# Joining the value products of an attention stage with the scores of the stage after next, in a kernel whose instruction order a planner writes

## The chip, the cores and the metric

The kernel runs on one core of one Trainium2 chip. The metric is the time of one execution on the device in microseconds (us); runs of one kernel are summed up by their median. A profiled execution gives, beside its own time, the span from the first to the last instruction and a record of each instruction on each engine.

## The reference

Local attention with block summaries, followed by a feed-forward network (FFN), all in float32:

```python
batch, n_heads, seq, head_dim = (4, 8, 768, 64); block, window = (32, 16)
k_sum = k.reshape(B, H, nb, block, D).max(axis=3)          # nb = 24 blocks
v_sum = v.reshape(B, H, nb, block, D).mean(axis=3)
scores_l = where(abs(pos_q - pos_k) < window, scale * q @ k.T, -1e9)
scores_s = scale * q @ k_sum.T + log(block)
a = softmax(concat([scores_l, scores_s]))
x = a @ concat([v, v_sum])                                  # 3072 tokens x 512
h = x @ w_in                                                # 512 -> 2048
out = (h * sigmoid(h)) @ w_out                              # 2048 -> 512
```

## The kernel before, in words

**Tiling.** The 3072 tokens make 24 attention *stages* of 128 tokens (`s`, six to a batch) and 12 FFN *chunks* of 256 tokens (`c`, two stages to a chunk). For each of the 16 slices `f` of the 2048 hidden columns a chunk has one product into the hidden layer (FFN1) and two out of it (FFN2, one per 128 tokens). Chunk 0 computes in float32 (FFN1 at L818, in halves at L840; FFN2 at L826). Later chunks split each operand in two float16 parts, an upper (`h`) and a lower (`l`), and add three products: FFN1 at L821, FFN2 at L829. Chunk 10 uses a scheme with seven instead of eight products of a block (L917, L948).

**An attention stage.** `job_scores` (L581) multiplies q and k into two PSUM banks (L594; in batch 0 L597 and L601 in float32). `job_a` masks and reduces on VectorE (L630), takes the exponential on ScalarE (L633), divides by the sum (L638 to L648), and turns the weights: in batch 0 by TensorE (L659) and a copy on ScalarE or VectorE (L234, L238, the lines of the helper `copy`), later by a DMA transpose (L680). `job_c` multiplies by the values into bank 7 (L712; L697 in batch 0), and `job_x` copies the result to `x`, the FFN's input (L728, L729; in chunk 0 by the helper `copy`). From stage 4 on, all scores go to the banks 6 and 3.

**Preparation.** For each batch from the second on, `job_k` and `job_scale` load k and q to find a scale (L369, L371, L389), `job_v` loads v for its block means and its maximum (L455, L457), and for each stage `job_qk` and `job_vs` load and convert q and k (L489 to L496) and v (L556 to L566). The loads go through three staging tiles `raw` in turn, so that the order in which jobs ask for a tile is the order in which loads become possible. The FFN's weights arrive packed; ScalarE and VectorE unpack them in chunk 0 (L754 to L760) and VectorE takes their maximum (L761). When the maxima of all slices are there, `w_scale` computes a scale: a transposition by TensorE (L784), six small steps on VectorE (L788 to L793), a broadcast by TensorE (L797) and a copy (`ws`, L798). Then `job_pair` converts two slices at once to the upper part (L774 on ScalarE, L775 on VectorE) and the lower part (L776). Chunk 1 can't begin its FFN1 before that.

**What sets the order.** None of these jobs issues its instructions at once. Each hands operations to `Plan` with the engines that can run them, an assumed cost for each, what they read and write, and an urgency. `Plan.schedule` simulates the five queues (TensorE, VectorE, ScalarE, GpSimd, and SyncE, which issues all DMAs) with these assumed costs, sweeps a few times backward and forward to find urgencies, and keeps the order that is shortest by its own account. That order is then issued, engine by engine; each engine works its queue in order and waits at an instruction whose inputs aren't there. `plan.slack` adds time to what an engine has to wait for by the plan. `TUNE` holds offsets of urgencies. Where the plan sees TensorE idle before chunk 0, or before an FFN1 block later, it inserts *fillers*, small bf16 products of an identity tile whose result nobody reads (L328).

## Time and profile before

| | us |
|---|---|
| median of 3 runs | 596.81 |
| lowest and highest run | 596.72, 597.51 |
| the profiled execution's own time | 597.37 |
| its span, first to last instruction | 595.7 |
| first float32 FFN1 matmul of chunk 0 (L840) starts | 24.90 |
| first float16 FFN1 matmul of chunk 1 (L821) starts | 88.55 |
| last matmul (L859) starts | 591.76 |

PE stands for TensorE's matmuls, PEld for its loads of weights, DVE for VectorE, ACT for ScalarE, POOL for GpSimd and SP for SyncE. In the rows of the timeline the first number is the start in us from the span's start, the second how long the group took, "x12" the number of instructions, and a bracket at the end the idle time before them and what ended it. Matmuls are pipelined, so that one is still recorded as busy while the next has begun: the distance from start to start tells what one costs. In a group's row the numbers behind the bar are the busy time of all in us and the mean of one in ns.

### The profile page before, as it was taken

How to read it: one execution, taken by the hardware profiler on the slowest of the kernel's cores; microseconds unless marked ns; L12 is line 12 of the kernel's file. 1: busy time of each engine (PE TensorE's matmuls, PEld its weight loads, DVE VectorE, ACT ScalarE, POOL GpSimd, SP SyncE). 2: the span in 40 equal slices, each digit the busy share in tenths (PEclk: the TensorE clock that was granted, in tenths of full speed). 3: DMA queues.
4: the chain of work that ended last, by engine and by line, in shares of the span. 5: the costliest groups of instructions: out<-in, count | busy, mean ns of one | idle time of the engine just before them, and what ended most of it. 6: DMA issues, size and time to landing. Idle time of an engine off the chain costs nothing.

```text
span 595.7 us, 15528 instructions
## 1 busy us (share of the span) xinstructions
PE 585.4 (98%) x5920; PEld 407.1 (68%) x5920; DVE 454.1 (76%) x1348; ACT 384.6 (65%) x1030; POOL 152.7 (26%) x221
## 2 busy tenths in 40 slices
PE   7999999999999999999999999999999999999997
PEld 5666656676676666666676766666666767788764
DVE  5999979998786848979895564988987896655432
ACT  4898849877766756647775643767876765533332
POOL 3211201035412000033331010236236637421000
PEclk9999999999999999999999999999999999999999
DMA  8999443125755633553555620344733321000000
GB/s 333 414 417 413 169 133 99 28 61 179 145 114 178 166 93 104 111 145 88 129 123 153 198 90 2 129 89 128 163 80 85 103 46 38 19 2 19 37 1 35
DMA packets 60918, 75.30 MB, mean 126 GB/s; under 512 B 41915, under 2 KB 42171, under 8 KB 59051
## 3 DMA queue, kind: packets, MB, share of 16 engines
q1 hardware_dynamic: 60842, 74.31, 42.3%
q8 instruction: 46, 0.75, 0.6%
q14 instruction: 30, 0.24, 0.1%
HBM read 56.79 MB, written 6.29 MB: 106 GB/s over the span
## 4 chain that ended last, share of the span: by engine, by line
PE 83%; DVE 9%; ACT 3%; DMA 3%; issue 1%; SPq 0%; ACTq 0%
PE bank L821 34%; PE bank L829 34%; PE bank L917 4%; PE bank L948 3%; PE bank L712 2%; PE bank L594 2%; DVE wm L761 2%; DVE wr L760 2%; DMA second<-in_qP_dram 1%; DVE e L630 1%; ACT wr L774 1%; DMA third<-first 1%; ACT wr L758 1%; PE bank L840 1%; DMA raw<-in_qF_dram 1%
## 5 line engine op out<-in xcount | busy, mean ns | idle before, releaser
L821 PE MATMUL bank<-x,wr 128*128 128x256 f16 x1920 | 234.6, 273 | 0.0
L821 PEld LDWEIGHTS <-wr 128*128 128x128 f16 x1920 | 186.7, 98 | 50.6 <-issue 0.6
L829 PE MATMUL bank<-wr,gh 128*128 128x512 f16 x638 | 190.1, 379 | 0.0
L845 ACT ACTIVATE t<-bank,th 128x256 f32<-128x256 f32 x160 | 75.0, 469 | 83.2 <-PE bank L821 82.3
L846 DVE SCALAR_TENSOR_TENSOR t<-t,bank 128x256 f32<-128x256 f32 x176 | 73.6, 418 | 68.8 <-ACT t L845 67.8
L829 PE MATMUL bank<-wr,gl 128*128 128x512 f16 x319 | 120.9, 379 | 0.2 <-DVE gl L849 0.2
L848 ACT ACTIVATE gh<-t 128x256 f16<-128x256 f32 x160 | 66.1, 414 | 52.6 <-DVE t L846 47.8
L849 DVE SCALAR_TENSOR_TENSOR gl<-t,gh 128x256 f16<-128x256 f32 x160 | 75.8, 474 | 24.1 <-ACT gh L848 23.0
L829 PEld LDWEIGHTS <-gh 128*128 128x128 f16 x638 | 60.0, 98 | 39.3
L633 ACT ACTIVATE e<-e,mx 128x120 f32<-128x120 f32 x192 | 73.1, 383 | 9.5 <-DVE mx L630 9.3
L829 PEld LDWEIGHTS <-gl 128*128 128x128 f16 x319 | 31.2, 98 | 39.2 <-DVE gl L849 2.1
L677 DVE SCALAR_TENSOR_TENSOR first<-e,sum,first 128x120 f16<-128x120 f32 x144 | 52.5, 411 | 0.0
L646 POOL TENSOR_SCALAR first<-e,sum 128x120 f16<-128x120 f32 x55 | 24.9, 462 | 96.5 <-ACT gh L848 29.8
L630 DVE CUSTOM_DVE_ANT_0 e<-bank,masks,qsc 128x120 f32<-128x120 f32 x144 | 42.0, 337 | 2.7 <-PE bank L594 2.7
L241 POOL TENSOR_TENSOR first<-raw,first 120x1024 f16<-120x1024 f32 x15 | 32.9, 2197 | 28.1 <-ACT first L234 27.2
L633 ACT ACTIVATION_READ_ACCUMULATOR e<-e,mx 128x1 f32 x192 | 36.4, 190 | 0.0
L826 PE MATMUL bank<-wr,t 128*128 128x512 f32 x64 | 30.7, 599 | 0.0
L646 POOL TENSOR_SCALAR e<-e,sum 128x120 f32<-128x120 f32 x28 | 11.2, 413 | 73.3 <-DVE sum L639 63.4
L241 POOL TENSOR_TENSOR wr<-wr 128x256 f32<-128x256 f32 x32 | 25.2, 808 | 12.5 <-DVE wr L897 8.0
L818 PE MATMUL bank<-x,wr 128*128 128x256 f32 x112 | 26.3, 379 | 0.0
L818 PEld LDWEIGHTS bank<-x,wr 128*128 128x128 f32 x112 | 21.0, 190 | 7.0 <-issue 4.1
L917 PE MATMUL bank<-x,wr 128*128 128x256 f16 x192 | 22.4, 273 | 0.4 <-DVE wr L923 0.4
(164 smaller groups left out, 757.0 us busy)
## 6 DMA issues: line engine op xcount, KB each, us to landing
wr<-in_w_dram SPq DMA_DIRECT2D x14, 1024.0 KB
raw<-in_qkT_dram SPq DMA_DIRECT2D x18, 576.0 KB
out_dram<-raw SPq DMA_DIRECT2D x23, 256.0 KB
raw<-in_kF_dram SPq DMA_DIRECT2D x12, 384.0 KB
raw<-in_qF_dram SPq DMA_DIRECT2D x9, 512.0 KB
raw<-in_vR_dram SPq DMA_DIRECT2D x12, 384.0 KB
raw<-in_v_dram SPq DMA_DIRECT2D x18, 208.0 KB
raw<-in_v_dram SPq DMA_DIRECT2D x18, 192.0 KB
```

Source lines behind the costliest of these rows:

```text
L241: eng[e].tensor_tensor(out=out, in0=in0, in1=in1, op=ALU.subtract)
L630: plan.op({"dve": 262 if b else 206}, lambda e, i=i, j=j, et=et, mx=mx: nc.vector.tensor_tensor_reduce(out=et[:, i, :], in0=sc[j][:, i, :N ...
L633: plan.op({"act": 385}, lambda e, i=i, j=j, et=et, mx=mx: nc.scalar.activation(out=et[:, i, :], in_=et[:, i, :], func=AF.Exp, scale=-1.0, ...
L677: nc.vector.scalar_tensor_tensor(out=pt[:, i, P:P + NKEY], in0=et[:, i, :], scalar=su4[:, 2 * j + i:2 * j + i + 1], in1=pt[:, i, :NKEY], o ...
L818: nc.tensor.matmul(out=h, lhsT=wi[:, ct * P:(ct + 1) * P], rhs=x0[:, ct, :], start=(ct == 0), stop=(ct == NCT - 1))
L821: nc.tensor.matmul(out=h, lhsT=wip[:, part, ct * P:(ct + 1) * P], rhs=x[:, ct, :], start=(ct == 0 and q == 0), stop=(ct == NCT - 1 and q = ...
L829: nc.tensor.matmul(out=bank[ob[u]], lhsT=g[:, u * P:u * P + P], rhs=wop[:, part, :], start=(opens and q == 0), stop=(closes and q == 2))
L845: plan.op({"act": 264 if c == 0 else 360}, lambda e: nc.scalar.activation(out=t, in_=h, func=AF.Tanh, scale=0.5 if c == 0 else th[:, 0:1]) ...
L846: plan.op({"dve": 337}, lambda e: nc.vector.scalar_tensor_tensor(out=t, in0=t, scalar=1.0, in1=h, op0=ALU.add, op1=ALU.mult), r=bk(k), w=[ ...
L848: plan.op({"act": 311}, lambda e: nc.scalar.activation(out=gh, in_=t, func=AF.Copy, scale=SHRINK), r=[("t", j)], w=[("gh", n)], prio=post)
L849: plan.op({"dve": 343}, lambda e: nc.vector.scalar_tensor_tensor(out=gl, in0=t, scalar=SHRINK, in1=gh, op0=ALU.mult, op1=ALU.subtract), r= ...
L917: nc.tensor.matmul(out=h, lhsT=wip[:, p, ct * P:(ct + 1) * P], rhs=x[:, ct, :], start=(ct == 0 and q == 0), stop=(ct == NCT - 1 and q == 2))
```

## The change

1. **Joined products.** For stages 6 to 21 without the last two of each batch (twelve stages), `job_c` adds the value products of stage `s` and the scores of stage `s + 2` as one operation, so that nothing comes between them on TensorE. To make that possible, the jobs of a stage are written in another order: `step` hands in the softmax of the next stage, the loads of the stage after next, the joined operation and the rest of the loads; and `job_scale` of batches 2 and 3 comes later than `job_k`.
2. **First conversions one slice each.** `job_pair` converts the slices 0 to 3 singly, the others in pairs as before; for a pair the plan now knows that FFN1 of its second slice waits for both of its conversions (`near`).
3. **Landings.** Operations on VectorE and ScalarE that read a freshly loaded tile (L369, L371, L455, L457, and the upper parts of q and k) are planned as if the load landed 1300 ns later.
4. **Urgencies.** `TUNE` has other values, and 72 `MOVES` are applied behind the sweeps: each draws random shifts for the urgencies of the operations in a stretch of the plan and sweeps once more. `Plan.move` was there before, with an empty list.

```diff
+LANDING = 1300
-MOVES = ()
+MOVES = ((258747, 243766, 16000, 300, 8), (489776, 214955, 2000, 1500, 1),
...
+SINGLE = 4
...
+    @contextmanager
+    def landing():
+        saved = plan.slack
+        plan.slack = dict(saved, **{e: max(LANDING, saved.get(e, 0)) for e in ("dve", "act")})
+        yield
+        plan.slack = saved
...
-        plan.op({"pe": 770}, mm, r=[ttk for _, ttk in parts] + [("v1", s % 2), ("v2", s % 2)], w=bk(7), prio=prio, cols=1536, mode=2)
+        need = [ttk for _, ttk in parts] + [("v1", s % 2), ("v2", s % 2)]
+        if not joined(s):
+            plan.op({"pe": 770}, mm, r=need, w=bk(7), prio=prio, cols=1536, mode=2)
+            return
+        go, more, homes = scores(s + 2)
+        plan.op({"pe": 1450}, lambda e: (mm(e), go(e)), r=need + more, w=bk(7) + homes, prio=prio, cols=2976, mode=2)
...
+        near = [("near", f0)] if n > 1 else []
...
-        need = [("wf", f, 0)] if c == 0 else [("wh", f, 0), ("wl", f, 0)]
+        need = [("wf", f, 0)] if c == 0 else [("wh", f, 0), ("wl", f, 0)] + ([("near", f - 1)] if c == 1 and f % 2 and f > SINGLE else [])
...
+    def joined(s):
+        return s >= NTILE and s % NTILE < NTILE - 2
...
+    def step(s):
+        end = B * NTILE
+        if s + 1 < end:
+            job_as(s + 1)
+        if s + 2 < end:
+            if s % NTILE == NTILE - 2:
+                job_scale(s // NTILE + 1, when(4 * s + 8) - TUNE["k"])
+            job_stage(s + 2, False)
+        job_cs(s, True)
+        if s + 2 < end:
+            if not joined(s):
+                job_scores(s + 2, when(4 * s + 8))
+            job_rest(s + 2)
...
         for kind in range(2):
-            job_pair((f, f + 1), kind, NFT + f + kind - TUNE["wp"])
+            for fs in ((f,), (f + 1,)) if f < SINGLE else ((f, f + 1),):
+                job_pair(fs, kind, NFT + f + kind - TUNE["wp"])
...
         if d and c and f == 0:
-            job_stage(2 * d)
-            job_attn(2 * d, True)
-            job_stage(2 * d + 1)
+            if c == 1:
+                for x in (2 * d, 2 * d + 1):
+                    job_stage(x)
+                    job_scores(x, when(4 * x))
+                    if x == 2 * d:
+                        job_as(x)
+            step(2 * d)
```

`scores` is the inner part of `job_scores`, which now returns the products, what they need and their banks; `job_as`, `job_cs` and `job_rest` are parts of `job_attn` and `job_stage` under names of their own.

**What it moves.** The order of the new kernel has other line numbers: L712 is L733 there, L594 L607, L821 L848, L829 L856, L818 L845, L826 L853, L234 L236, L754 L780, L758 L784, L633 L651, L845 L872, L846 L873, L457 L468, L455 L466, L447 L457, L788 to L793 L815 to L820, L798 L825, L774 to L776 L801 to L803, L328 L330 (and L840 for the fillers of an FFN1 block). `first` holds the values, `second` q and k, `third` the turned weights.

On TensorE, before, an attention stage's scores (here those of stage 8) follow an FFN2 product:

```order
L829 LDWEIGHTS gl0_174
L829 MATMUL bank4_182<-wr_61,gl0_174 128x512
L594 LDWEIGHTS second_122
L594 MATMUL bank6_184<-second_122 64x120
L594 LDWEIGHTS second_122
L594 MATMUL bank3_181<-second_122 64x120
```

Now the same scores follow the last value products of stage 6:

```order
L733 LDWEIGHTS first_121
L733 MATMUL bank7_185<-third_123,first_121 64x64
L607 LDWEIGHTS second_122
L607 MATMUL bank6_184<-second_122 64x120
L607 LDWEIGHTS second_122
L607 MATMUL bank3_181<-second_122 64x120
```

So one change between FFN tiles and small tiles is gone; the order has this step twelve times.

On ScalarE, before, at the end of the start phase: copies of turned weights (`third`), the block means (`wr<-vms`), unpacking of FFN weights (`wr<-wr`), and divisions (`e<-e,sum`):

```order
L234 COPY third<-bank_180 120x256
L234 COPY wr<-vms 24x512
L234 COPY third<-bank_181 120x256
L234 COPY wr<-vms 24x512
L758 ACTIVATE wr<-wr 128x512
L644 ACTIVATE e_159<-e_159,sum_151 128x120 x2
L754 ACTIVATE wr<-wr 128x512
L758 ACTIVATE wr<-wr 128x512
L234 COPY third<-bank_183 120x256
L758 ACTIVATE wr<-wr 128x512
L754 ACTIVATE wr<-wr 128x512 x2
```

Now, with a copy of the attention's result to `x` that VectorE had before, and the tanh of the first FFN tile at the end:

```order
L662 ACTIVATE e_158<-e_158,sum_151 128x120
L236 COPY wr<-vms 24x512 x2
L236 COPY third<-bank_183 120x256
L780 ACTIVATE wr<-wr 128x512
L784 ACTIVATE wr<-wr 128x512 x3
L651 ACTIVATE e_160,sum_148<-e_160,mx_154 128x120 x2
L236 COPY x_164<-bank_185 128x4x128
L651 ACTIVATE e_161,sum_148<-e_161,mx_155 128x120 x2
L784 ACTIVATE wr<-wr 128x1024
L872 ACTIVATE t_166<-bank_178 128x256
```

All unpacking has moved behind the last copy of turned weights, and the copy to `x` stands behind four steps of it. On TensorE the scores of a stage that stood behind the second block of L697 stand ahead of it now.

On VectorE, before, around the scale of the FFN's weights (`wc`, `ws`), with the two reductions of v (`am`, `vm`) of the next batch:

```order
L789 TENSOR_SCALAR wc<-wc 1x2
L457 TENSOR_REDUCE am<-raw_119 128x1
L790 TENSOR_SCALAR wc<-wc 1x2
L455 TENSOR_REDUCE vm<-raw_119 128x24
L791 TENSOR_SCALAR wc<-wc 1x2
L846 SCALAR_TENSOR_TENSOR t_168<-t_168,bank_178 128x256
L792 RECIPROCAL wc<-wc 1x2
L793 SCALAR_TENSOR_TENSOR wc<-wc 1x1
L846 SCALAR_TENSOR_TENSOR t_169<-t_169,bank_179 128x256
L798 COPY ws<-bank_184 128x4
L447 TENSOR_TENSOR th_146<-ws,vsc_140 128x2
L775 TENSOR_SCALAR wr<-wr,ws 128x2x512 x2
```

Now:

```order
L819 RECIPROCAL wc<-wc 1x2
L820 SCALAR_TENSOR_TENSOR wc<-wc 1x1
L873 SCALAR_TENSOR_TENSOR t_168<-t_168,bank_178 128x256
L466 TENSOR_REDUCE vm<-raw_119 128x24
L468 TENSOR_REDUCE am<-raw_119 128x1
L825 COPY ws<-bank_184 128x4
L457 TENSOR_TENSOR th_146<-ws,vsc_140 128x2
L802 TENSOR_SCALAR wr<-wr,ws 128x512 x2
L803 SCALAR_TENSOR_TENSOR wr<-wr,ws 128x512
L802 TENSOR_SCALAR wr<-wr,ws 128x512
```

The reductions have left the chain of the small steps and stand ahead of the copy of the scale; the first conversions are of one slice (512 columns) instead of two.

More of the change, by code (lines that the diff above doesn't have):

```diff
@@ L2 @@
 import random
-from contextlib import ExitStack
+from contextlib import ExitStack, contextmanager
 import concourse.bass as bass
@@ L601, in go, with job_scores @@
                             nc.tensor.matmul(out=bank[both[u]][side[z], hp * P:hp * P + NKEY][:, means[z]], lhsT=q0_t[s % NQ0][rows, hp, side[z]], rhs=km0[rows, hp], start=True, stop=True)
+        need = [(x, s % 2) for x in ("qh", "ql", "kh", "kl", "km2")] if b else [("q0", s % NQ0)] + [(x, hp) for x in ("k0", "k0m") for hp in range(4)]
+        return go, need, bk(both[0]) + bk(both[1])
+    def job_scores(s, prio):
+        b, both = s // NTILE, score_banks(s)
+        go, need, homes = scores(s)
         if s < 2:
@@ L1015, in job_stage, with job_rest @@
                 job_mean(-TUNE["v0"])
-        job_vs(s, p[0] - TUNE["vs"] if b else p[0])
+        if rest:
+            job_rest(s)
+    def job_rest(s):
+        b, t = divmod(s, NTILE)
+        p = when(4 * s)
+        job_vs(s, p - TUNE["vs"] if b else p)
         if t == (4 if b else 5) and b + 1 < B:
```

58 lines of the change are left out of this document (35 added, 23 removed).

## Prediction

> **What bounds the kernel now.** I read the page first, then the windows, then what TensorE waited for, then the timeline at each place where it waited. The busy line of the page, three windows (us, busy us of PE, PEld, DVE, ACT, POOL, granted clock, DMA share, GB/s) and TensorE's own list of waits (us in total, times, longest):
>
> ```profile
> PE 585.4 (98%) x5920; PEld 407.1 (68%) x5920; DVE 454.1 (76%) x1348; ACT 384.6 (65%) x1030; POOL 152.7 (26%) x221
> 25.00:50.00 25.00, 25.00 (x109) 17.83 (x110) 23.88 (x51) 23.51 (x45) 2.47 (x7) 1.00 1.02 419
> 75.00:100.00 25.00, 23.64 (x174) 15.08 (x173) 20.84 (x52) 17.55 (x41) 0.00 (x0) 1.00 0.35 113
> 110.00:120.00 10.00, 10.00 (x69) 6.52 (x68) 10.00 (x22) 7.14 (x16) 0.00 (x0) 1.00 0.01 2
> 450.00:500.00 50.00, 50.00 (x581) 34.01 (x581) 39.08 (x115) 34.20 (x97) 31.71 (x37) 1.00 0.28 63
> PE bank L597 <- ACT raw L874: 1.0, 1, 1.0
> PE bank L697 <- ACT third L234: 0.8, 1, 0.8
> PE bank L917 <- DVE wr L923: 0.4, 1, 0.4
> PE bank L797 <- DVE wc L793: 0.4, 1, 0.4
> ```
>
> TensorE is busy for 98% of the span at a granted clock of 1.00, so nothing is to be had from the clock. From 100 us on it is gapless but for 0.4 us (L917). All that a new order can take back lies in three places: the first 25 us, before the first FFN matmul; three waits between 65 and 92 us (0.8 + 0.4 + 1.0 = 2.2 us); and what TensorE spends inside its busy time on work that isn't products. The set of products is unchanged by the change, so that last part is the cost of changing from one shape of tile to another, and of fillers.
>
> **Part one: joined values and scores.** Around one block of scores (L594, 64x64 tiles) and one of values (L712, 120x64 tiles) the timeline reads (start, us, engine, line):
>
> ```profile
> 186.13 0.38 PE L829 MATMUL bank<-wr,gh 128*128 128x512 f16 x1
> 186.35 0.38 PE L829 MATMUL bank<-wr,gl 128*128 128x512 f16 x1
> 186.66 0.82 PE L594 MATMUL bank<-second 64*64 64x120 f16 x48
> 187.42 1.81 PE L821 MATMUL bank<-x,wr 128*128 128x256 f16 x15
> ...
> 271.86 0.38 PE L829 MATMUL bank<-wr,gl 128*128 128x512 f16 x1
> 272.17 0.95 PE L712 MATMUL bank<-third,first 120*64 120x64 f16 x48
> 273.05 0.50 PE L821 MATMUL bank<-x,wr 128*128 128x256 f16 x3
> ...
> L712 PE MATMUL bank<-third,first 120*64 120x64 f16 x864 | 17.1, 197 | 0.0
> ```
>
> One L829 follows another after 0.22 us (186.13 to 186.35), but a block of small tiles follows an L829 only after 0.31 us (186.35 to 186.66, 271.86 to 272.17): entering costs 0.09 us, for scores and for values alike. A value block then holds TensorE for 0.88 us (272.17 to 273.05). Its 48 matmuls start over 0.95 - 0.20 = 0.75 us, some 0.02 us apart, so leaving costs 0.88 - 0.75 - 0.02 = 0.11 us. Before, a stage pays both entries and both exits. Joined, the entry into the scores from an FFN block goes for certain: 0.09 us. The step from 120x64 to 64x64 tiles has no row of its own for f16; it costs between nothing (then 0.11 us more is saved) and as much as the exit that it replaces. I take the exit's cost, since the shape of the tile changes there too. Twelve stages are joined (four in each of three batches): 12 x 0.09 = **-1.1 us**; bounds -1.1 and 12 x 0.20 = -2.4 us. [...]
>
> What the joined step adds: the scores of stage s+2 now stand right behind the values of stage s in TensorE's queue. They need the converted q and k of stage s+2, and both score banks read out by stage s+1. Were they late, all FFN blocks behind them would wait. I cost that at nothing, because two stages of FFN work lie between the joins and a wait of this kind isn't in the list above; it is the second rival.
>
> **Part two: the start.** From 19 us to the first FFN output product (L826):
>
> ```profile
> 21.28 0.66 ACT L754 ACTIVATE wr<-wr 128x512 uint32<-128x512 uint32 x1
> 21.84 0.71 ACT L758 ACTIVATE wr<-wr 128x512 f32<-128x512 f32 x1
> 22.43 0.34 ACT L234 COPY third<-bank 120x256 f32<-120x256 f32 x1
> 21.79 1.49 PE L697 MATMUL bank<-third,wr 120*64 120x64 f32 x32
> 23.20 0.40 PE L597 MATMUL bank<-first,second 64*64 64x96 f32 x8
> 24.90 2.94 PE L840 MATMUL bank<-x,wr 128*128 128x128 f32 x24
> 26.99 0.38 ACT L845 ACTIVATE t<-bank 128x256 f32<-128x256 f32 x1 [0.45 <-PE bank L840]
> 27.41 0.41 DVE L846 SCALAR_TENSOR_TENSOR t<-t,bank 128x256 f32<-128x256 f32 x1
> 29.08 1.88 PE L826 MATMUL bank<-wr,t 128*128 128x512 f32 x4
> 23.36 0.67 DVE L238 COPY x<-bank 128x512 f32<-128x512 f32 x1
> ...
> L633 ACT ACTIVATE e<-e,mx 128x120 f32<-128x120 f32 x192 | 73.1, 383 | 9.5 <-DVE mx L630 9.3
> L758 ACT ACTIVATE wr<-wr 128x1024 f32<-128x1024 f32 x14 | 16.3, 1164 | 0.0
> ```
>
> ScalarE has three steps of unpacking FFN weights (an L754 of 0.66 and two L758 like that of 21.84, 0.71: together 2.1 us) ahead of the last copy of attention weights (22.43) that stage 1's values (L697) wait for. The new order puts them behind that copy, and the scores block of 23.20 to 24.90 ahead of those values, where TensorE had been filling time. So the copy can end at 22.77 - 2.1 = 20.7, the values run from 20.8 to 21.9, and the first L840 starts at about 22.0 instead of 24.9. But the copy of stage 1's result to x moves from VectorE (23.36) to ScalarE, behind one L754, three L758 and two exponentials: 0.66 + 3 x 0.71 + 2 x 0.38 = 3.5 us, then 0.6 for the copy itself: 20.7 + 4.1 = 24.8. The second half of the L840s (two of four blocks of 2.94 / 3 = 1.0 us) waits for it and completes the first tile at 25.8. Then ScalarE has two exponentials and a wide L758 (1.16 us) ahead of the tanh, which starts at 26.7; with 0.38 + 0.41 us for tanh and product, L826 comes at 27.5 instead of 29.08: **-1.5 us**. Bounds: nothing (weights converted later, as VectorE at 23.88 of 25 us has no room), and the whole 2.9 us of the first L840.
>
> **Part three: the waits of 65 to 92 us.** VectorE, TensorE and ScalarE around the scale of the weights:
>
> ```profile
> 79.66 0.16 DVE L789 TENSOR_SCALAR wc<-wc 1x2 f32<-1x2 f32 x1
> 81.27 0.95 DVE L457 TENSOR_REDUCE am<-raw 128x1 f32<-128x768 f32 x1 [1.46 <-DMA raw<-in_vR_dram]
> 83.65 0.15 DVE L793 SCALAR_TENSOR_TENSOR wc<-wc 1x1 f32<-1x1 f32 x1
> 83.85 0.38 PE L797 MATMUL bank<-wc,ones 1*128 1x4 f32 x2 [0.36 <-DVE wc L793]
> 84.26 0.16 DVE L798 COPY ws<-bank 128x4 f32<-128x4 f32 x1
> 85.64 1.42 DVE L775 TENSOR_SCALAR wr<-wr,ws 128x1024 f16<-128x1024 f32 x2 [1.02 <-ACT wr L774]
> 86.97 6.31 DVE L776 SCALAR_TENSOR_TENSOR wr<-wr,ws 128x1024 f16<-128x1024 f32 x5
> 88.55 1.47 PE L821 MATMUL bank<-x,wr 128*128 128x256 f16 x12
> ```
>
> The six small steps from L788 to L793 last 4 us because two reductions of v (0.95 us each) stand between them, the first with 1.46 us of waiting for its load. The new order moves both behind L793, where they run beside the FFN block and the three L826 products that TensorE has between L784 and L797; so the 0.4 us at L797 go. From the copy of the scale (L798) to the first fp16 product 4.3 us pass now (84.26 to 88.55), with the upper parts of two pairs (1.42) and the lower part of one (6.31 / 5 = 1.26) ahead of it on VectorE. With one f each these are 2 x 0.36 and 0.63: with the copy 0.16 + 0.72 + 0.63 = 1.5 us. TensorE's own cover for it shrinks from five L826 products to three, six matmuls of 1.88 / 4 = 0.47 us by row 29.08, 2.8 us: enough, so no new wait comes in its place: **-0.4**. The wait of 0.8 at L697 has about the same cover as before (two L826 products, 1.9 us, instead of one FFN block), but ScalarE now has its copies in a row there: **-0.8**. At L597 (1.0) the eviction of the second bank on ScalarE still has conversions ahead of it, now two of one f instead of one of a pair, so I take half: **-0.5**. Sum **-1.7 us**, bounds 0 and -2.2.
>
> **Part four: what comes in its place.** The new order has four fillers ahead of one FFN block of chunk 1, where before had none after the start:
>
> ```profile
> 8.86 2.47 PE L328 MATMUL bank<-ident 128*128 128x256 bf16 x21
> ```
>
> They are 2.47 / 21 = 0.12 us each, 0.5 us. VectorE is busy for 10.00 of 10 us at 110 to 120, so when TensorE arrives some 3 us earlier, conversions can't all be earlier too; I add one wait like that of L917, 0.4 us, and round to **+0.8 us**, bounds 0 and +3.2 (all that parts two and three gain). The moves of urgencies and the 1.3 us allowed for landings shift work on engines that have idle time (VectorE 24%, ScalarE 35%) once chunk 1 is over, at 39.08 and 34.20 of 50 us; behind 130 us I cost them at nothing, cover being TensorE's own queue. If that cover is gone, it is the second rival again. The last block and the stores behind it are unchanged.
>
> Sum: -1.1 - 1.5 - 1.7 + 0.8 = -3.5 us. On the profiled execution's own 597.37 us that is 593.9; the median of the runs is 596.81, 0.56 lower, and gives **593.3 us**. The difference that a measurement of this kernel can tell from none is about 0.2%, 1.2 us: faster means under 595.6, slower over 598.0.
>
> **Rivals.**
> - *VectorE becomes the bound in chunk 1.* For it: 10.00 of 10 us, and 23.88 of 25 during chunk 0. Against it: 20.84 of 25 us from 75 to 100, of which 1.46 is the wait that goes. Then parts two and three (3.2 us) are given back but for about a third, and the result is -1.1 - 1.0 + 0.8 = -1.3: 595.5 us.
> - *The joined scores wait, slower.* Place: TensorE at the step from values to scores. Price: the upper and lower part of k are one conversion on ScalarE (0.82 us) and one on VectorE (0.92), rows below; if the load lands late these 1.7 us stand after it, the value block hides 0.75, so 1.0 us shows. It decides from 3.5 / 12 = 0.3 us a join on; at six of twelve joins it is +6.0 - 3.5 = +2.5: 599.3 us. For it: ScalarE already waits for that load (0.6 us in all). Against it: TensorE waits for none of these conversions now.
> - *All goes through.* Parts two and three at 2.5 and 2.2, no new wait: -1.1 - 2.5 - 2.2 = -5.8: 591.0 us, and 1.3 less where the step between small tiles is free.
> - *The change doesn't do what it says* falls: the order shows values and scores without a row between them.
>
> ```profile
> L492 ACT ACTIVATE second<-raw,qsc 128x640 f16<-128x640 f32 x15 | 12.3, 818 | 0.7 <-DMA raw<-in_qkT_dram 0.6
> L494 DVE SCALAR_TENSOR_TENSOR second<-raw,qsc,second 128x640 f16<-128x640 f32 x18 | 16.6, 922 | 0.5 <-ACT second L492 0.4
> ```
>
> **The numbers.** Forecast 0.57 (its own range 591.8 to 594.9), VectorE bound 0.20, joins wait 0.11, all goes through 0.12. Faster takes the forecast, all of the third and under half of the first rival (those below 595.6): 0.57 + 0.12 + 0.08 = 0.77; the rest of the first, 0.12, is the same; slower 0.11. The range reaches from the third rival with half of the free step (591.0 - 0.6) to joins alone with the fillers (596.81 - 1.1 + 0.5): 590.4 to 596.2, and leaves out the slower rival and the ends of the others.
>
> **What would show it.** Right: a first L840 near 22 and a first L826 near 27.5; no wait at L797 and L697; first fp16 product at about 85.5 instead of 88.55; 0.9 us from a joined block's first value to its first score. Free step: 0.77 us there. Wrong: waits of TensorE for second (q, k) or for score banks at the joins, or a list of TensorE's waits behind 92 us that sums to more than 2 us; or a start that moves by under 0.5 us.

## The result and the profile after

| | before | after |
|---|---|---|
| median of six runs, us | 596.87 | 601.47 |
| lowest and highest run, us | 596.19, 597.51 | 599.85, 602.21 |
| the profiled execution's own time, us | 597.37 | 599.85 |
| its span, us | 595.7 | 598.1 |
| first FFN2 product of chunk 0 starts | 29.08 | 28.27 |
| first FFN2 product of chunk 1 starts | 95.22 | 92.15 |
| from there to the last matmul starts | 496.55 | 502.10 |

The kernel became slower: ratio 1.007 [1.0056, 1.0084]. The forecast of 593.3 us and its range up to 596.2 both missed. Three of the six runs of after had a mean granted clock of 0.997 and were on average 1.6 us longer than the other three; the profiled one is the fastest, so what follows explains its 2.48 us (599.85 - 597.37) and not the whole distance of the medians. Of the experiments below, one execution of e6 (675.01 us) and one of e9 (865.34 us) ran at a mean granted clock of 0.849 and 0.657 and are left out of their medians and ratios.

The last three rows of the table split the change in two: up to chunk 1 the kernel gained 95.22 - 92.15 = 3.07 us, near the 3.2 us forecast for start and early waits together; behind it, it lost 502.10 - 496.55 = 5.55 us where the forecast had a gain of 0.3 (1.1 for the joins less the 0.8 of part four, whose fillers stand at 122 us and whose wait was expected at 110 to 120). So 5.55 + 0.3 = 5.85 us are to be found behind 92 us, most of them in a stretch that the prediction called covered. The page's busy line, two windows (columns as in the prediction) and TensorE's own list of waits:

```profile
PE 584.6 (98%) x5921; PEld 407.1 (68%) x5921; DVE 463.2 (77%) x1366; ACT 382.3 (64%) x1027; POOL 139.2 (23%) x214
175.00:190.00 15.00, 13.91 (x171) 8.24 (x170) 14.26 (x54) 11.80 (x43) 4.21 (x6) 1.00 0.45 125
526.00:546.00 20.00, 16.75 (x145) 13.95 (x144) 9.72 (x22) 7.51 (x15) 4.42 (x8) 1.00 0.04 15
PE bank L944 <- DVE wr L950: 1.8, 2, 0.9
PE bank L944 <- ACT wr L949: 1.3, 1, 1.3
...
PE bank L856 <- DVE gl L876: 1.0, 3, 0.5
...
PE bank L406 <- DVE qm L400: 0.6, 1, 0.6
PE bank L856 <- ACT gh L875: 0.2, 1, 0.2
```

Before, both windows were full (15.00 of 15 and 20.00 of 20 us). TensorE's busy sum hardly moved, 585.4 to 584.6, but it now stands idle at two new places: chunk 10 (L944 is L917 of before) for 3.25 of 20 us, and around 175 to 190 us for 1.09 of 15. By the list the waits behind 92 us sum to 1.8 + 1.3 + 1.0 + 0.6 + 0.2 = 4.9 us, over the 2 us that the prediction had named as the sign that it is wrong.

More names of the new order: L948 is L975, L922 (tanh of chunk 10) L949, L923 (its product) L950, L848 and L849 (upper and lower part of the hidden layer) L875 and L876, L840 is L867, L697 is L718, L630 is L648, L494 is L507; L677 of before (lower part of the softmax's result) is L695; L238 and L240 are VectorE's copies.

**The joins** came as forecast. The timeline of TensorE around one:

```profile
167.94 0.95 PE L733 MATMUL bank<-third,first 120*64 120x64 f16 x48
168.82 0.82 PE L607 MATMUL bank<-second 64*64 64x120 f16 x48
```

From the first value to the first score 168.82 - 167.94 = 0.88 us pass, at all twelve joins alike. The six value blocks that an FFN product still follows take the same 0.88, so the step from 120x64 to 64x64 tiles costs as much as the exit that it replaces, 0.11 us by the prediction's reckoning (0.88 - 0.75 - 0.02), and isn't free. No join waits.

**Chunk 10.** The timeline of before and then of after, TensorE with ScalarE and VectorE between:

```profile
519.74 2.78 PE L917 MATMUL bank<-x,wr 128*128 128x256 f16 x24
522.36 2.46 PE L948 MATMUL bank<-wr 128*128 128x256 f16 x21
522.62 0.47 ACT L922 ACTIVATE wr<-bank,th 128x256 f32<-128x256 f32 x1 [1.56 <-PE bank L917]
523.13 0.42 DVE L923 SCALAR_TENSOR_TENSOR wr<-wr,bank 128x256 f32<-128x256 f32 x1 [1.34 <-ACT wr L922]
```

```profile
528.93 0.46 ACT L949 ACTIVATE wr<-bank,th 128x256 f32<-128x256 f32 x1
529.44 1.47 PE L944 MATMUL bank<-x,wr 128*128 128x256 f16 x12 [1.29 <-ACT wr L949]
531.01 0.42 DVE L950 SCALAR_TENSOR_TENSOR wr<-wr,bank 128x256 f32<-128x256 f32 x1 [1.21 <-PE bank L944]
...
535.71 1.47 PE L944 MATMUL bank<-x,wr 128*128 128x256 f16 x12 [0.94 <-DVE wr L950]
...
543.18 2.02 PE L944 MATMUL bank<-x,wr 128*128 128x256 f16 x17 [0.89 <-DVE wr L950]
```

L944 makes hidden slices in the two halves of one PSUM bank. Before, from 508 us on, both halves (24 matmuls) were always written in one go, and the 21 L948 matmuls behind them gave ScalarE and VectorE 2.3 us to read both out. Now the groups are cut in two: a half is written while the engines still hold the other half of the same bank, and TensorE waits (1.29, 0.94 and 0.89 us in the rows above; that the shared bank is the cause, e2 shows). In the row of 531.01 VectorE waits 1.21 us for TensorE, and in that of 529.44 TensorE 1.29 us for ScalarE: they pass one bank to and fro. The order of TensorE's rows says the same (from 519.74 us before and from 524.72 us after):

```
before: L917 x24, L948 x21, L917 x24, L948 x21, L917 x24, L948 x21
after:  L944 x24, L856 x3, L944 x12, L975 x9, L944 x12, L975 x12, L944 x12, L975 x9, L944 x24, L975 x12, L944 x24, L975 x45
```

**175 to 190 us.** VectorE, GpSimd and TensorE in the timeline of after:

```profile
169.32 3.33 DVE L695 SCALAR_TENSOR_TENSOR first<-e,sum,first 128x120 f16<-128x120 f32 x2
...
176.14 0.41 DVE L876 SCALAR_TENSOR_TENSOR gl<-t,gh 128x256 f16<-128x256 f32 x1
169.05 1.26 POOL L238 TENSOR_SCALAR first<-raw 120x1024 f16<-120x1024 f32 x1 [0.35 <-ACT gh L875]
170.39 2.12 POOL L243 TENSOR_TENSOR first<-raw,first 120x1024 f16<-120x1024 f32 x1
176.61 0.39 PE L856 MATMUL bank<-wr,gl 128*128 128x512 f16 x1 [0.34 <-DVE gl L876]
```

A pair of L695 takes 0.60 us elsewhere (at 164.15); this one takes 3.33. Its first half (1.12) lies over GpSimd's copy L238 and its second (2.29) over GpSimd's subtraction L243 (170.39 to 172.51). The softmax L648 that follows, and the L876 for which TensorE waits at 176.61, come later for it.

Such a pair is not new. The timeline of before has one as long (L677 is L695, L241 is L243), and another of 3.29 us at 300.19:

```profile
273.50 3.35 DVE L677 SCALAR_TENSOR_TENSOR first<-e,sum,first 128x120 f16<-128x120 f32 x2
274.58 2.13 POOL L241 TENSOR_TENSOR first<-raw,first 120x1024 f16<-120x1024 f32 x1
```

TensorE doesn't wait behind either of them. What the new order changed is where such a pair falls and how much work TensorE has left at that moment.

### The profile page after: what moved, and what is told of

It reads as the page before. It is cut to its first block, busy times and chain, and to the rows that moved or that the text cites. A ratio compares the mean times of both kernels' runs of the same rounds, so it can differ in the third digit from the quotient of the medians.

```text
span 598.1 us, 15525 instructions
## 1 busy us (share of the span) xinstructions
PE 584.6 (98%) x5921; PEld 407.1 (68%) x5921; DVE 463.2 (77%) x1366; ACT 382.3 (64%) x1027; POOL 139.2 (23%) x214
## 4 chain that ended last, share of the span: by engine, by line
PE 84%; DVE 10%; ACT 3%; DMA 1%; issue 1%; SPq 0%; DVEq 0%; ACTq 0%
PE bank L856 31%; PE bank L848 30%; PE bank L853 4%; PE bank L845 4%; PE bank L944 4%; PE bank L975 2%; PE bank L733 2%; DVE e L648 2%; DVE first L695 2%; PE bank L607 2%; DVE wr L803 1%; PE bank L718 1%; DMA second<-in_qP_dram 1%; DVE gl L876 1%; DVE t L873 1%
## 5 line engine op out<-in xcount | busy, mean ns | idle before, releaser
L848 PE MATMUL bank<-x,wr 128*128 128x256 f16 x1920 | 233.2, 273 | 0.0
L848 PEld LDWEIGHTS <-wr 128*128 128x128 f16 x1920 | 187.2, 98 | 49.5 <-issue 0.6
L856 PE MATMUL bank<-wr,gh 128*128 128x512 f16 x638 | 190.1, 379 | 0.3 <-ACT gh L875 0.2
L856 PE MATMUL bank<-wr,gl 128*128 128x512 f16 x319 | 121.0, 379 | 1.0 <-DVE gl L876 1.0
L872 ACT ACTIVATE t<-bank,th 128x256 f32<-128x256 f32 x160 | 74.2, 465 | 66.0 <-PE bank L848 65.9
L873 DVE SCALAR_TENSOR_TENSOR t<-t,bank 128x256 f32<-128x256 f32 x176 | 72.5, 413 | 51.3 <-ACT t L872 50.3
L875 ACT ACTIVATE gh<-t 128x256 f16<-128x256 f32 x160 | 66.0, 413 | 55.7 <-DVE t L873 51.3
L876 DVE SCALAR_TENSOR_TENSOR gl<-t,gh 128x256 f16<-128x256 f32 x160 | 75.8, 475 | 29.5 <-ACT gh L875 28.6
L856 PEld LDWEIGHTS <-gh 128*128 128x128 f16 x638 | 60.5, 98 | 43.4 <-ACT gh L875 1.3
L651 ACT ACTIVATE e<-e,mx 128x120 f32<-128x120 f32 x192 | 73.3, 384 | 20.5 <-DVE mx L648 20.4
L856 PEld LDWEIGHTS <-gl 128*128 128x128 f16 x319 | 31.2, 98 | 41.2 <-DVE gl L876 4.4
L695 DVE SCALAR_TENSOR_TENSOR first<-e,sum,first 128x120 f16<-128x120 f32 x144 | 51.6, 404 | 0.2 <-ACT first L662 0.2
L648 DVE CUSTOM_DVE_ANT_0 e<-bank,masks,qsc 128x120 f32<-128x120 f32 x144 | 41.4, 333 | 1.8 <-PE bank L607 1.7
L651 ACT ACTIVATION_READ_ACCUMULATOR e<-e,mx 128x1 f32 x192 | 36.3, 189 | 0.0
L243 POOL TENSOR_TENSOR first<-raw,first 120x1024 f16<-120x1024 f32 x14 | 30.9, 2207 | 3.2 <-ACT first L236 2.6
L853 PE MATMUL bank<-wr,t 128*128 128x512 f32 x64 | 30.8, 599 | 0.0
L243 POOL TENSOR_TENSOR wr<-wr 128x256 f32<-128x256 f32 x32 | 25.1, 799 | 22.0 <-DVE wr L924 13.8
L664 POOL TENSOR_SCALAR e<-e,sum 128x120 f32<-128x120 f32 x33 | 13.6, 427 | 70.2 <-DVE sum L657 61.4
L845 PEld LDWEIGHTS bank<-x,wr 128*128 128x128 f32 x112 | 21.2, 190 | 7.6 <-issue 4.8
L845 PE MATMUL bank<-x,wr 128*128 128x256 f32 x112 | 26.1, 379 | 0.0
L944 PE MATMUL bank<-x,wr 128*128 128x256 f16 x192 | 22.9, 272 | 3.3 <-DVE wr L950 1.8
```

What stands on the lines that cost most here:

```text
L243: eng[e].tensor_tensor(out=out, in0=in0, in1=in1, op=ALU.subtract)
L648: plan.op({"dve": 262 if b else 206}, lambda e, i=i, j=j, et=et, mx=mx: nc.vector.tensor_tensor_reduce(out=et[:, i, :], in0=sc[j][:, i, :N ...
L651: plan.op({"act": 385}, lambda e, i=i, j=j, et=et, mx=mx: nc.scalar.activation(out=et[:, i, :], in_=et[:, i, :], func=AF.Exp, scale=-1.0, ...
L695: nc.vector.scalar_tensor_tensor(out=pt[:, i, P:P + NKEY], in0=et[:, i, :], scalar=su4[:, 2 * j + i:2 * j + i + 1], in1=pt[:, i, :NKEY], o ...
L845: nc.tensor.matmul(out=h, lhsT=wi[:, ct * P:(ct + 1) * P], rhs=x0[:, ct, :], start=(ct == 0), stop=(ct == NCT - 1))
L848: nc.tensor.matmul(out=h, lhsT=wip[:, part, ct * P:(ct + 1) * P], rhs=x[:, ct, :], start=(ct == 0 and q == 0), stop=(ct == NCT - 1 and q = ...
```

## The experiments

Three theories stood at first. **A**: about 4 us of the loss are chunk 10's cut groups, through the one bank. **B**: VectorE has become the bound from chunk 1 on, 463.2 us busy against 454.1. **C**: the joined scores wait, or upset what follows. Later came **P**, that VectorE loses time where GpSimd's v subtraction runs beside it, and for the start **F**, that TensorE waits for its own instructions. Each time is the median of 6 to 12 runs, each ratio is against the kernel before on the same chip. The experiments ran on four chips, on which the kernel before took 597.23 us (e1 to e4), 596.66 (e5 to e7), 596.82 (e8 to e10) and 596.46 (e11, e12); from one group to another compare the ratios, not the times.

**e1, chunk 10's urgencies left alone.** The shifts of `MOVES` stop short of chunk 10:

```diff
-            self.prio[i] += by.setdefault(i // block, rng.gauss(0, size))
+            self.prio[i] += by.setdefault(i // block, rng.gauss(0, size)) * (i < self.tail)
```

> The changed kernel with its 72 shifts drawn as before, but not added to the operations of chunks 10 and 11; the order is the changed kernel's up to the first products of chunk 10, and from there each pair of first FFN products is followed by 21 second ones again. Theory A (the loss is in chunk 10, where the shifts part the two halves of a pair): the waits of 1.29, 0.94 and 0.89 us at the first products of chunk 10 go, the median falls from 601.5 to 596.5-597.5, about the kernel before. Theory B (VectorE is late in chunks 1 to 3) and theory C (the joined blocks cost more than they save): the tail gives back under 1 us, 600.5-601.5.

Measured 596.75 us, ratio 0.9986 [0.9967, 1.0006]. Its timeline has the old groups again, 24 of L944 and 21 of L975 in turn, and no wait there:

```profile
526.53 2.78 PE L944 MATMUL bank<-x,wr 128*128 128x256 f16 x24
```

For A. But the profiled execution (598.63 us, 1.9 above the median) has a stall that after doesn't have, although up to 508 us all engines issue the rows of after in the same order:

```profile
135.94 2.42 POOL L243 TENSOR_TENSOR first<-raw,first 120x1024 f16<-120x1024 f32 x1 [1.16 <-ACT first L236]
136.30 2.75 DVE L507 SCALAR_TENSOR_TENSOR second<-raw,qsc,second 128x640 f16<-128x640 f32 x1
142.50 0.39 PE L856 MATMUL bank<-wr,gl 128*128 128x512 f16 x1 [1.44 <-DVE gl L876]
```

It is a matter of timing, to which e8 comes back; with it in the profile, e1 doesn't settle A alone.

**e2, the order of after with two banks.** Every engine issues the rows of after in the same order; only the second half of a chunk's hidden slices goes to another bank, from slice 5 on (free at that time):

```diff
-        h, hk = bank[0][:, n * CH:n * CH + CH], [("bank", 0, n)]
+        h, hk = bank[1 if n and f > 4 else 0][:, n * CH:n * CH + CH], [("bank", 0, n)]
```

> The changed kernel in its own order, instruction for instruction; only the odd halves of the first FFN products of chunk 10 from slice 5 on lie in bank 1 instead of the other half of bank 0. If TensorE waits there because the two halves share a bank (a reader of one half is waited for before the other half is written, and the reverse), the three waits of 1.29, 0.94 and 0.89 us go: 3.1 us less, 598-598.5 at the median, or 597 if a dip of the clock goes with them. If it waits for the chain tanh, product, sums itself, or for the accumulators, nothing changes: 601-601.7.

Measured 596.67, ratio 0.9994 [0.9974, 1.0014]; the cut groups now run without a wait:

```profile
528.41 1.47 PE L944 MATMUL bank<-x,wr 128*128 128x256 f16 x12
529.72 1.15 PE L975 MATMUL bank<-wr 128*128 128x256 f16 x9
530.71 1.47 PE L944 MATMUL bank<-x,wr 128*128 128x256 f16 x12
```

That shows A: from the first FFN2 product of chunk 1 to the last matmul it takes 498.17 us instead of 502.10, and TensorE's rows of the two traces drift apart by these 3.9 us in chunk 10 alone. So the one bank costs 3.9 us. It also shows what A leaves: 498.17 is still 1.9 us above the 496.25 that the forecast had for this stretch (496.55 - 1.1 + 0.8).

**e3, less work on VectorE.** The order of after; the reductions of k and v read an eighth of their elements, so that this kernel leaves out most of what its scales and block means are made from:

```diff
-...in_=kf.rearrange("p (n k) -> p n k", k=BLK), axis=AX.X, op=ALU.max),
+...in_=kf.rearrange("p (n k) -> p n k", k=BLK)[:, :, :4], axis=AX.X, op=ALU.max),
...
-...in_=vr, axis=AX.X, op=ALU.max, apply_absolute_value=True)
+...in_=vr[:, :96], axis=AX.X, op=ALU.max, apply_absolute_value=True)
```

> The changed kernel in its own order; the twelve reductions a batch on VectorE that find block maxima of k, sums of v and the maximum of v read an eighth of their columns, so VectorE has some 5 us less to do in each batch's lead; what they leave out makes the scales and means wrong. Theory B (VectorE is the bound in chunks 1 to 3): the waits at 100-104 us (0.9) and 175-188 us (1.6) go, 599.0 at the median. Theory A: those waits come from the order around them, not from these reductions, or what is gained there is lost again; 601-601.5.

Measured 601.05, ratio 1.0064 [1.0044, 1.0085]: nothing gained. The waits at 186 to 188 us went, but others came at 141.49 (1.32 us) and 177.78 (0.70). The first is the stall of e1 again: a VectorE conversion (L503, at 134.43) lasts 2.65 us beside the v subtraction, where it takes 0.86 in after. So less work moved the timing as well, and e3 alone can't tell B from P; e6 and e8 can.

**e4, the joins alone.** No moves, no landings, pairs of two slices, the old offsets of urgencies:

```diff
-LANDING = 1300
+LANDING = 0
-MOVES = ((258747, 243766, 16000, 300, 8), (489776, 214955, 2000, 1500, 1),
...
+MOVES = ()
-SINGLE = 4
+SINGLE = 0
```

> The joined blocks alone: the table of 25 numbers of the kernel before, no shifts, no landing slack, no single conversions. The forecast's first term: 12 exits of 0.09 us, 1.1 us less than the kernel before, 595.8. Theory C (the scores wait behind the values in the joined block, from 0.3 us a join): 600-603. Theory A says nothing against the first term: under 597.

Measured 600.95, ratio 1.0053 [1.0032, 1.0074], far over the 595.8 expected (the 0.09 us named there are the entries of the scores). No join waits here either, so C falls as the prediction's rival had put it. This order has a loss of its own, though; its timeline and windows:

```profile
147.25 1.01 PE L856 MATMUL bank<-wr,gh 128*128 128x512 f16 x2 [2.42 <-ACT second L505]
...
146.45 0.74 DVE L902 TENSOR_SCALAR raw<-bank,th 128x512 f32<-128x512 f32 x1
```

```profile
145.00:147.00 2.00, 0.00 (x0) 0.00 (x0) 2.00 (x9) 2.00 (x9) 0.00 (x0) 0.96 0.18 71
147.00:150.00 3.00, 2.58 (x43) 1.29 (x45) 3.00 (x13) 2.16 (x8) 0.00 (x0) 0.50 0.45 175
```

The chunk's first FFN2 product waits 2.42 us, by the times for the bank that VectorE's L902 still has to read out (to 147.19); the releaser named by the row had long been done. Then the granted clock is 0.50, up to about 153.7 us, which by estimate costs more than the wait: half of the 6.4 us from 147.25 on, 3.2 us. Without these two the stretch from chunk 1's first FFN2 product to the last matmul, 501.20 us in e4, would be near 495.6, and the joins alone were forecast to give 495.45 (496.55 - 1.1). So e4 doesn't speak against the first term, and doesn't show it either.

**e5, VectorE's copy ahead of the unpacking in the start** (two banks as in e2). In the start phase of after the copy to `x` on VectorE, which sets free the bank of the second value block, stands behind two shifts that wait for loads:

```profile
20.01 0.43 DVE L782 TENSOR_SCALAR wr<-wr 128x512 uint32<-128x512 uint32 x1 [0.62 <-DMA wr<-in_w_dram]
21.28 0.43 DVE L782 TENSOR_SCALAR wr<-wr 128x512 uint32<-128x512 uint32 x1 [0.84 <-DMA wr<-in_w_dram]
21.62 0.69 DVE L240 COPY x<-bank 128x512 f32<-128x512 f32 x1
...
22.41 1.15 PE L718 MATMUL bank<-third,wr 120*64 120x64 f32 x32 [0.91 <-issue]
24.60 3.84 PE L867 MATMUL bank<-x,wr 128*128 128x128 f32 x32 [1.03 <-DVE sc L443]
```

The planned order is rearranged before it is issued (`shifts` are those two, `dve[at]` is the copy):

```diff
+        plan[at:at] = shifts
+        at = plan.index(dve[[o[2] for o in dve].index(self.copied) + 1]) + 1
+        plan.insert(at, unpack)
```

> The kernel with the two banks, and VectorE's order at the start changed by hand: the copy of x ahead of the two shifts of weight bits that wait for their loads, and the second joining of bits ahead of four softmax steps. The forecast's part two went wrong by VectorE's order there: the second block of value products starts at 21.5 instead of 22.7 us, the first FFN product at 23.3-23.5 instead of 24.7, the first second product near 27.2 instead of 28.4, and the time falls by 1.0-1.3 us, to 595.4-595.7 beside 596.7. Rival: the load of the weights or ScalarE's copy of the second half of x sets that start: the first FFN product at 24.2 or later, under 0.5 us.

Measured 597.83, ratio 1.0008 [0.9994, 1.0022], no gain over e2. Its profile has the stall of e1 too (1.42 us at 142.43), so its time says little of the start. In it the second value block did start earlier, and the first FFN product didn't (24.83, against 24.68 in e2):

```profile
21.65 1.15 PE L729 MATMUL bank<-third,wr 120*64 120x64 f32 x32
24.83 3.84 PE L879 MATMUL bank<-x,wr 128*128 128x128 f32 x32 [2.03 <-DVE sc L455]
21.60 1.29 DVE L798 SCALAR_TENSOR_TENSOR wr<-wr 128x512 uint32<-128x512 uint32 x2
```

By these rows the unpacked weights that the product needs were there at 22.9 at the latest, so that what TensorE waits for until 24.83 seems not to be VectorE, whatever the bracket names. Nor is it ScalarE's copy to `x`: in e2 that copy ends at 24.77, behind the product's start. F was formed here.

**e6, less work on GpSimd** (two banks). From stage 8 on GpSimd's v subtraction (L243) does 64 of 512 columns and leaves out the lower parts of the others; the order is the same:

```diff
-        plan.op({"pool": 2180, "dve": 1135}, lambda e: less(e, v2a, va, v1a), ...
+        plan.op({"pool": 2180, "dve": 1135}, lambda e: less(e, v2a[..., :64], va[..., :64], v1a[..., :64]) if e == "pool" and s > 7 else less(e, v2a, va, v1a), ...
```

> The kernel with the two banks, in its own order; GpSimd's subtraction that makes the low parts of the values (2.1 us) takes only 64 of 512 columns from stage 8 on, so the low parts of the rest are stale. Theory P (VectorE's subtractions at 169-172 and 181 us, 1.96 and 1.54 us longer than usual, stand still while GpSimd runs, and that makes the gelu parts late): those instructions take their usual 0.3 us, the waits of TensorE at 175-176 us (0.6) and 186-188 us (1.0) go, the time falls by 1.2-1.6 us to 595.1-595.5. Theory B (VectorE has too much to do there, GpSimd or not): the waits stay, 596.4-596.9.

Measured 593.88, ratio 0.9961 [0.9938, 0.9984]. The same two places in its timeline, and the window of 175 to 190 us:

```profile
169.35 1.64 DVE L695 SCALAR_TENSOR_TENSOR first<-e,sum,first 128x120 f16<-128x120 f32 x2
174.49 0.41 DVE L876 SCALAR_TENSOR_TENSOR gl<-t,gh 128x256 f16<-128x256 f32 x1
170.43 0.43 POOL L243 TENSOR_TENSOR first<-raw,first 120x128 f16<-120x128 f32 x1
```

```profile
175.00:190.00 15.00, 15.00 (x188) 10.15 (x186) 13.82 (x55) 12.71 (x43) 2.61 (x6) 1.00 0.52 121
```

The pair of L695 loses 1.7 us of its length (what is left over its 0.60 lies over the copy L238, which e6 keeps), L876 comes 1.65 us earlier, the window is full. The 18 blocks of scores behind 130 us tell where the time comes from: against e2 they start 0.21 us earlier at 169, 2.03 at 205 and 2.26 at 467, so 1.8 of the 2.4 us (498.17 - 495.76) fall between 169 and 205 us. For P, and against B: VectorE had the same operations to do, GpSimd less.

**e7, no moves** (`MOVES = ()`, everything else of after).

> The changed kernel without its 72 shifts (the joined blocks, the new table of 25 numbers, the landing slack and the single conversions stay). Theory A (the shifts broke chunk 10, their work ahead of it is good): pairs of chunk 10 are whole, no waits there, but the start and the waits of 65-92 us come back in part: 595-598. If the shifts did the harm all over: under 594.5. If they did more good than harm: over 600.

Measured 597.77, ratio 1.0009 [0.9992, 1.0025]. Without the moves chunk 10 is whole, and the rest takes 498.91 us: the moves cost the 3.9 us of chunk 10 and elsewhere bring some 0.7 (498.91 to e2's 498.17). What is left above the 496.25 of the forecast, 2.7 us, is not the moves' doing; which other part of the change brings it wasn't separated.

**e8, VectorE and GpSimd held apart** (two banks, the full computation). The plan keeps such pairs apart in its own time, but nothing holds them apart on the chip. Ahead of each v subtraction but the first two, which no lower part precedes, GpSimd now reads one element of what VectorE's last lower part (L695) has written, and so waits for it:

```diff
+            if e == "pool" and i in self.after_low:
+                if last_low is not None:
+                    self.after_low[i](last_low)
...
+        plan.after_low[len(plan.ops)] = lambda pt: nc.gpsimd.tensor_scalar(out=stop_t, in0=pt[:1, 0, P:P + 1], scalar1=1.0, scalar2=0.0, op0=ALU.mult, op1=ALU.add)
```

> The kernel with the two banks; ahead of each of GpSimd's subtractions for the values stands one GpSimd instruction of a single element that reads what VectorE's last low-part subtraction ahead of it in the plan's order wrote, so that GpSimd starts behind it as planned. The full computation. Theory P (VectorE stands still while GpSimd runs; the plan keeps the two apart in its own time, the chip only where a wait does): VectorE's instructions at 169-172 and 181 us take their usual 0.3 us, TensorE's waits at 175-188 us shrink from 1.6 us to under 0.5, 594.7-595.7 beside 596.7. Theory B: 596.4-597.

Measured **593.90**, ratio 0.9949 [0.9930, 0.9968]: faster than both kernels. Its timeline (L703 is L695, L656 is L648, L248 is L243, L586 the one element):

```profile
173.09 0.58 DVE L703 SCALAR_TENSOR_TENSOR first<-e,sum,first 128x120 f16<-128x120 f32 x2
174.20 0.33 DVE L656 CUSTOM_DVE_ANT_0 e<-bank,masks,qsc 128x120 f32<-128x120 f32 x1
173.51 0.22 POOL L586 TENSOR_SCALAR stop<-first 1x1 f16<-1x1 f16 x1 [0.61 <-DMA third<-first]
173.69 2.12 POOL L248 TENSOR_TENSOR first<-raw,first 120x1024 f16<-120x1024 f32 x1
```

The one element starts at 173.51, behind the first of the pair, which wrote it (the bracket names a DMA). The pair takes 0.58 us, GpSimd's 2.12 us now lie over L656, which reads a PSUM bank and takes 0.33 us, the mean of L648 in after. P is shown: with all the work done and only these two engines' order tied, no lower part lies over a v subtraction any more (their mean is 0.36 us for 0.41 in e2), and the stretch behind chunk 1's first FFN2 product takes 496.17 us, 2.0 less than in e2.

P also accounts for the stalls of e1, e3 and e5 near 140 us. There a conversion on VectorE began just behind the v subtraction (136.30 to 135.94 in e1) and lasted 2.65 to 2.75 us; in after and e2 the same conversion began ahead of it (L507 at 134.94, L243 at 135.64 in after) and took 0.87. Nothing in these kernels orders the two, in e8 neither, so a shift of about 1 us decides, and that after's profile shows no loss there is luck.

**e9 to e12, the start.** In e9 (on e5) the early fillers are made in pairs twice as wide, 48 instructions of TensorE fewer; e10 is e9 with e8's order; e11 zeroes the fillers' tile by VectorE first; e12 also puts ScalarE's second copy to `x` ahead of two exponentials.

```diff
+            wide = 0 if self.ops[i][6] else fills // 2
+            for n in range(fills - wide):
+                (self.wide if n < wide else self.ops[i][6] or self.fill)()
...
+    plan.wide = lambda: nc.tensor.matmul(out=bank[0], lhsT=both[:, :P], rhs=both, start=True, stop=True)
...
+        at = next(k for k, o in enumerate(act) if o[2] == self.second)
+        exps = [o for o in act[at - 2:at]]
...
+        plan[at:at] = exps
```

> The kernel with VectorE's start changed by hand, and the filler products ahead of the first FFN products made in pairs of 512 columns instead of 256, so that TensorE has some 48 instructions fewer ahead of the first FFN product, at the same work. In nine traces so far that product starts 2.25 to 2.83 us after the start of a 16 KB instruction fetch at 21.5-22.9 us, while what it waits for (VectorE's first joining of bits, 22.3 us here) is long done. Theory F (TensorE has no instructions until that fetch lands): the first FFN product starts at 22.9-23.5 us instead of 24.8, the first second product at 27.2-27.6 instead of 28.5, the time falls by 0.8-1.2 us against the same kernel with narrow fillers (597.4-597.8): 596.4-597. Rival (something else holds it, the copy of the second half of x on ScalarE for one): 24.4 or later, no gain.

Measured 598.40, ratio 1.0021 [1.0006, 1.0036]: the tile came from GpSimd only at 5.75 us, and the start slipped by 3 us. But the idle time ahead of the first FFN product is gone (values from 24.68, product at 25.76).

> Two banks, GpSimd behind VectorE, VectorE's start changed by hand and wide fillers together, the full computation. If theories A, P and F hold and their gains add: 593.5-594.7, faster than both kernels. If only A and P hold: 594.7-595.7. If P fails: 596.4 or more.

Measured 596.04, ratio 0.9982 [0.9966, 0.9997]; the late tile again.

> As the kernel with all three, but the tile that the wide fillers read is set to zero by VectorE as its first instruction, not by GpSimd behind its masks, so the fillers start near 1.5 us as they do in the kernel before, instead of 5.75. Theory F (the stall ahead of the first FFN product is TensorE's instruction fetch, and 48 instructions fewer move its boundary behind that product): the first FFN product at 22.8-23.3 us, no idle time between it and the value products, the first second product at 27.2-27.7, the time 592.5-593.4, about 1 us under the kernel with GpSimd behind VectorE alone (593.9). Rival: it stands at 24.4 or later again, 593.7-595.

Measured 594.34, ratio 0.9957 [0.9942, 0.9972]:

```profile
23.00 1.15 PE L743 MATMUL bank<-third,wr 120*64 120x64 f32 x32
24.08 1.16 PE L893 MATMUL bank<-x,wr 128*128 128x128 f32 x8
25.85 2.94 PE L893 MATMUL bank<-x,wr 128*128 128x128 f32 x24 [0.61 <-ACT x L253]
```

No idle time between values and product (24.08 - 23.00 = 1.08 us for 32 matmuls), but the values came 0.6 us later than in after. The first scores at 6.7 to 9.4 us ran slower (L634, 0.58 to 0.60 us a group, where after has 0.37 to 0.40); what slowed them was not shown. There is also a wait for ScalarE's copy, and at 24.08 the product lies outside the 22.8 to 23.3 that F had forecast.

> As the one before, and ScalarE copies the second half of x ahead of two exponentials instead of behind them. If that copy is what comes late once the fetch does not (0.6 us of idle time at the fifth FFN product in the kernel with all three): 0.4-0.6 us less than the one before, 592.0-593.0. If the exponentials' delay of 0.56 us comes back at the next scores: no difference.

Measured **592.68**, ratio 0.9937 [0.9923, 0.9951], the fastest of all, 3.8 us (596.46 - 592.68) under the kernel before on its chip. The wait is gone: its L900, the first FFN products, run 32 without a break.

```profile
23.82 1.15 PE L749 MATMUL bank<-third,wr 120*64 120x64 f32 x32
24.90 4.00 PE L900 MATMUL bank<-x,wr 128*128 128x128 f32 x32
```

The intervals of e8, e11 and e12 overlap, so a gain of the new start over e8 isn't shown.

## Why the prediction was wrong

| stretch | before | after | e2 | e6 | e8 | e12 |
|---|---|---|---|---|---|---|
| to chunk 1's first FFN2 product, us | 95.22 | 92.15 | 92.45 | 92.17 | 94.40 | 93.42 |
| from there to the last matmul | 496.55 | 502.10 | 498.17 | 495.76 | 496.17 | 495.90 |

The columns of e8 and e12 are from executions of 596.2 and 594.96 us, each 2.3 above its median. In e8 the granted clock is 0.50 for some 3.4 us from 26 us on, which by estimate lengthens its first row by half of that, 1.7 us; in e12 the page has 8 tenths of the full clock in the first 14.83 us.

- **The step that failed** is the sentence "behind 130 us I cost them at nothing, cover being TensorE's own queue". It argued from free shares of whole engines, and the two losses don't come from shares. In chunk 10 the moves cut groups whose point was to be whole, and TensorE's queue is itself what waits: 3.9 us (e2). And where VectorE stalls beside GpSimd, TensorE now runs out of L876: 2.0 (e8) to 2.4 us (e6), 1.2 and 1.8 of them between 169 and 205 us. The stall itself is in before too, where TensorE's queue did cover it. The sum, 5.9 to 6.3, is close to the 5.85 us looked for. The order was compared at the start and at the scale of the weights only; the one row that counts here, 24 and 21 matmuls in turn before, was in it.
- **Its own sign** of being wrong, waits behind 92 us over 2 us in sum, came true at 4.9. The other sign, a start moved by under 0.5 us, came true for the first FFN1 product (24.90 to 24.60, 0.30 where 2.9 was forecast) and not for the first FFN2 product (0.81).
- **Part one** was right in mechanism: no wait at the joins, the step between small tiles paid in full (0.11 us, as assumed). With both losses removed the rest takes 495.76 and 496.17 us against the forecast 496.25, which lets the -1.1 and the +0.8 of part four stand together; the time of neither was measured by itself.
- **Part two** forecast -1.5 us and brought -0.81 (29.08 to 28.27). The step followed ScalarE's queue: its copy did come early (19.50). But the second value block waits for VectorE's copy, behind two shifts that wait for loads (e5), and the first product came at 24.60, not 22.0. About 1 us of that is idle time of TensorE behind inputs that seem to be there (e5), and its cause stays open (F, below). ScalarE's copy to `x` ended at 24.48, near the 24.8 forecast.
- **Part three** forecast -1.7; with 3.07 in all and 0.81 of it in the start, it brought 2.26, the upper bound of 2.2: all three waits are gone. The first float16 product came at 86.86, where about 85.5 was named; the rest was gained between it and chunk 1's first FFN2 product.
- **Part four**: one wait of 0.55 us between chunk 1 and the rest (L406 at 103.82, waiting for VectorE), near the 0.4 allowed. It stands in the trace of every kernel here but before and e7, and its cause was not tried. Before wasn't quite gapless behind 100 us but for L917 either: it has one more wait of 0.22 us at 284.50, which changes nothing here.
- **The rivals**: VectorE as the bound falls, since e6 and e8 remove the waits and leave VectorE its operations; joined scores that wait don't occur; "all goes through" (591.0) isn't reached even by e12, which at 592.68 is nearer to the forecast of 593.3, and only with five edits that the change doesn't have. No rival named the bank of chunk 10 or GpSimd beside VectorE, though both were in the code: the plan names that bank and keeps these two engines apart in its own time.

What stays open: about 2 of the 4.6 us between the medians, which the profiled execution with its 2.48 doesn't show. Two things on record would fit, and neither was tried on after itself. In e4 and e8 a wait was followed by a granted clock of 0.50 (below); a mean of 0.997 over 598 us is 3.6 us at 0.50, which by estimate costs 1.8 us, near the 1.6 that after's executions at 0.997 took longer. And the stall near 140 us can fall into executions of after as it did into e5's profile, where it cost 1.74 us against e2.

## What to carry to other kernels

Ask of a new order not only which engines have time left but which groups it cuts: here a producer that filled one bank in two halves waited for its readers, and a second bank gave 3.9 us back (e2). A planner that keeps two engines apart in its own time has promised nothing on the chip; where one was slow beside the other, a wait that ties them (0.22 us of GpSimd at 173.51) gave 2.0 us back (e8). And cost a shift "of nothing" only after reading its rows in the order wherever the old order was a strict pattern.

## What the runs showed of the hardware

- **VectorE beside GpSimd.** Beside GpSimd's v subtraction (2.12 us in after, 2.42 in e1) two VectorE instructions lasted long: the second L695 of a pair in after 2.29 us, where the median of all 144 is 0.33, and e1's L507 2.75 us, where after's at 134.94 takes 0.87. In e1 the subtraction began 0.36 us ahead of L507 (135.94 and 136.30); where L507 began 0.70 us ahead of it, in after (134.94 and 135.64), it was short. At the pair in after the two starts (170.36 and 170.39) lie too close to tell which came first. L656 in e8, which reads a PSUM bank, keeps its 0.33 beside the subtraction. Why the one is slowed and the other isn't was not shown.
- **The clock after a wait.** In e4 2.42 us of waiting (to 147.25) are followed by a granted clock of 0.50 up to about 153.7, nearly 7 us. In e12 TensorE waits 2.6 us ahead of the first scores, and the page's clock is 8 tenths in the first of its 40 slices (14.83 us) and 9 in every other. In the profile of e8 1.85 us of waiting (to 24.94) are followed by a clock of 0.50 to 0.51 from 26 to 29 us (the window of 26 to 27):

```profile
26.00:27.00 1.00, 1.00 (x7) 1.00 (x7) 0.01 (x2) 0.00 (x0) 1.00 (x4) 0.51 0.96 401
```

  After the 2.03 us of e5 at the same place the clock stays at 1.00 in every window from 20 to 32 us, so the length of one wait doesn't decide it alone; what does was not shown.
- **Instructions of TensorE.** In after, e1, e2, e3, e5, e6 and e8 TensorE is idle for 0.8 to 2.0 us ahead of the first FFN product, whatever VectorE's order is. In after a 16 KB read of instructions (queue q8 of the DMA view) begins at 22.24 us, 2.36 us ahead of the product (24.60), while the DMA engines move 408 GB/s (22 to 24 us); in e5 one such read lies between 22 and 23.4 us (427 GB/s), the product at 24.83. In before, e4 and e7 no wait ahead of that product is listed, so that they tell nothing of it. With 48 instructions fewer (e9 to e12) the idle time is gone, and in e12 no such read lies between 22 and 25 us, the product at 24.90. But in e9, e11 and e12 the values end later too, and the product of e12 is no earlier than that of after. So that the number of instructions matters, and that TensorE waits for that read, are inferred from the times and not shown; an experiment that moves the read alone wasn't made. Of the 46 such reads in after four begin in the first 50 us (11.77, 22.24, 28.55 and 50.00), where the DMA engines move 404, 408, 389 and 418 GB/s (the 2 us from 11, 22, 28 and 49), and such idle time stands behind one of them alone.
